# Bounding a MoE-style layer's weights with products of TensorE, and giving their halves three free places

## The chip, the core and the metric

The kernel runs on one core of a Trainium2 chip. TensorE (PE) multiplies, VectorE (DVE) and ScalarE (ACT) do elementwise work and reductions, GpSimd (POOL) does elementwise work too, SyncE (SP) issues the DMAs. The metric is the time of one execution in microseconds (us).

## What is computed

```python
q_n, k_n, c_n = q, k, centroids divided by (their norms + 1e-6)
q_assign = argmax(q_n . c_n);  k_assign = argmax(k_n . c_n)      # 16 clusters per head
scores = where(q_assign == k_assign, (q @ k.T) / sqrt(D), -1e9)
attn   = softmax(scores)
x      = (attn @ v) laid out as (B*S, H*D) = (3072, 512)
r      = maximum(x @ moe_w_in, 0)                                # moe_w_in (512, 2048), float64
out    = (s * r * r + b) @ moe_w_out                             # moe_w_out (2048, 512), float64
```

B = 4, H = 8, S = 768, D = 64. Attention within clusters, then a two-layer MLP with a squared Relu. The weights and `s`, `b` lie in memory as 64-bit floats, so each weight is two 32-bit words.

## The kernel before

The work is a list of 192 attention **units** (one batch, one chunk of 256 queries, one pair of heads, one of two query tiles, one head) and 192 **MLP steps** (batch, chunk, one of 16 slices `ft` of the hidden layer). Unit `i` makes scores on TensorE (`scores`, L454), their maximum on VectorE (`maxima`, L463, tile `ssm`), the exponentials on ScalarE (`exps`, L473, tile `p`), the 16-bit high and low parts `ph` (L119 or L121, and L496 on GpSimd), a transpose by DMA (`PT`), and for each pair of units the product with the values (`values`, L515 to L517, tile `px`), then normalised into `xs` (L527). The first 8 units have no low part and are turned by TensorE (`turned`, L493). MLP step `m` runs 21 units behind (`LAG`): `mlp_in` (L573, tile `h`), `mlp_relu` (L580 to L583, tiles `r`, `g`), `mlp_gl` (L588), `mlp_out` (L600, tile `acc`). `mlp_start` computes per chunk a scale `cf` (L562) from the largest `xs`; each Relu needs it.

The products run in 16 bit with every operand split in a high and a low part, and for the weights that needs a bound first. The weights come in 32 **halves** of 128 x 512 numbers (`wi0`, `wo0`, `wi1`, `wo1`, ... `wo15`; even ones from `moe_w_in`, odd ones from `moe_w_out`). The generator `weights` moves each half through these steps, two per unit:

- `fetch`: DMA of 512 KB into a staging tile `wst`, one of three; the next load into the same tile waits until the half in it is joined.
- `rebase` (ScalarE, L203): makes a 32-bit float out of the high words, short of three bits.
- `narrow` (VectorE): shifts these words left by three (L207) and joins the top three bits of the low words (L208).
- `bound`: ScalarE writes the absolute values in 16 bit (`wab`, L215 or L217). For odd halves it also sums them by row (`l1`). For even halves TensorE multiplies them by ones (`pw`, L220), which sums the columns, and VectorE takes the largest (`w1`, L221).

`finish_w_in` and `finish_w_out` make scales in `glob` out of the bounds. Then `wsplit(ft)` splits each half into a 16-bit high part on ScalarE (L265, tiles `wis`, `wos`) and a low part on VectorE (L267). The split goes into a new place of the ring of `weight_tile`, and the place of the unsplit half is free only once its low part is made. The ring has 33 places for 32 halves.

Within each engine instructions run in the order of a list that a scheduler writes when the program is built, on its own estimates of durations; the first 20 units have a raised priority. So a change of one operation can move others in these lists.

Of the kernel before, what the change touches and what calls it, by code (L numbers as in the profile page):

```python
# [9 lines left out]
BF16 = mybir.dt.bfloat16  # L10
F32 = mybir.dt.float32
I32 = mybir.dt.int32
U32 = mybir.dt.uint32
AF = mybir.ActivationFunctionType
ALU = mybir.AluOpType
AX = mybir.AxisListType
# [10 lines left out]
def tile_cluster_attention_mlp(ctx, tc, q, k, v, cent, w_in, w_out, s_in, b_in, out):  # L27
# [28 lines left out]
    def const(shape, dt, name):  # L56
        return cp.tile(shape, dt, tag=name, name=name)

    def floor2(eng, dst, src):
        eng.tensor_scalar(dst, src, 2.0 ** -60, 2.0 ** 60, op0=ALU.max, op1=ALU.min)  # L60
        eng.tensor_scalar(dst.bitcast(I32), dst.bitcast(I32), EXPMASK, None, op0=ALU.bitwise_and)

    def inverse2(eng, dst, src, e):
        eng.tensor_scalar(dst.bitcast(I32), src.bitcast(I32), -1, (254 + e) << 23, op0=ALU.mult, op1=ALU.add)
# [25 lines left out]
    def columns(n, name):  # L90
        return sb.tile([P, n], BF16, tag=f"amb{n}", name=f"amb_{name}", bufs=3)
# [12 lines left out]
    rev = const([P, C], F32, "rev")  # L104
    for c in range(C):
        G.memset(rev[:, c : c + 1], float(C - c))
    ones = const([P, P], BF16, "ones")
    G.memset(ones, 1.0)
    ident = const([P, P], F32, "ident")
    G.memset(ident, 1.0)  # L110
    G.affine_select(ident, ident, pattern=[[1, P]], base=0, channel_multiplier=-1, compare_op=ALU.is_equal, fill=0.0)
    identb = const([P, P], BF16, "identb")
# [53 lines left out]
    WSP = {}  # L166

    def weight_tile(name):
        return cp.tile([P, KT, P], F32, tag="w", name=name, bufs=2 * NF + 1)
    w1 = const([P, NF], F32, "w1")  # L170
    l1 = const([P, NF], F32, "l1")
    glob = const([P, 12], F32, "glob")
    bias = []

# [26 lines left out]
    def rebase(d):  # L201
        hw = d["st"][:, :, :, 1].bitcast(F32)
        A.activation(d["w"], hw, AF.Prelu, scale=2.0 ** -112, alpha=-(2.0 ** 32))  # L203

    def narrow(d):
        c = d["w"].bitcast(I32)
        V.tensor_scalar(c, c, 3, None, op0=ALU.logical_shift_left)  # L207
        V.scalar_tensor_tensor(c.bitcast(U32), d["st"][:, :, :, 0].bitcast(U32), 29, c.bitcast(U32),  # L208
                               op0=ALU.logical_shift_right, op1=ALU.bitwise_or)

    def bound(d):
        w, p, ft = d["w"], d["p"], d["ft"]
        wa = sb.tile([P, KT, P], BF16, tag="wab", name=f"wab_{p}", bufs=2)
        if p % 2:
            A.activation(wa, w, AF.Abs, accum_out=l1[:, ft : ft + 1])  # L215
        else:
            A.activation(wa, w, AF.Abs)  # L217
            pw = ps_h.tile([P, 512], F32, tag="h", name=f"pw_{ft}")
            for t in range(KT):
                nc.tensor.matmul(pw[:, :P], ones, wa[:, t, :], start=(t == 0), stop=(t == KT - 1))  # L220
            V.tensor_reduce(w1[:, ft : ft + 1], pw[:, :P], axis=AX.X, op=ALU.max)  # L221
        if ft == NF - 1:
            (finish_w_out if p % 2 else finish_w_in)()

    narrowed = [0]

    def weights():
        live = {}
        for i in range(2 * NF + 3):
            if 0 <= i - 3:  # L230
                bound(live[i - 3])
                narrowed[0] += 1
            if 0 <= i - 2 < 2 * NF:
                rebase(live[i - 2])
                narrow(live[i - 2])
            if i < 2 * NF:
                live[i] = fetch(i)
            if i < 2 * NF + 2:
                yield

    def finish_w_in():
        V.tensor_reduce(glob[:, 0:1], w1, axis=AX.X, op=ALU.max)
        V.tensor_scalar(glob[:, 0:1], glob[:, 0:1], 1.02, None, op0=ALU.mult)
        floor2(V, glob[:, 1:2], glob[:, 0:1])
        inverse2(V, glob[:, 2:3], glob[:, 1:2], 0)
        V.tensor_scalar(glob[:, 2:3], glob[:, 2:3], 2.0 ** 13, None, op0=ALU.mult)
        V.tensor_scalar(glob[:, 1:2], glob[:, 1:2], 2.0 ** -7, None, op0=ALU.mult)

    def finish_w_out():
        lc = columns(1, "w")  # L250
        V.tensor_reduce(lc, l1, axis=AX.X, op=ALU.max)
        allmax(glob[:, 4:5], lc, "w")
        floor2(V, glob[:, 4:5], glob[:, 4:5])
        inverse2(V, glob[:, 5:6], glob[:, 4:5], 0)
        V.tensor_scalar(glob[:, 5:6], glob[:, 5:6], 2.0 ** 13, None, op0=ALU.mult)
        V.tensor_scalar(glob[:, 4:5], glob[:, 4:5], 2.0 ** -13, None, op0=ALU.mult)
        V.tensor_tensor(glob[:, 6:7], sv, glob[:, 4:5], op=ALU.mult)

    def wsplit(ft):
        while narrowed[0] < 2 * NF:  # L260
            next(wgen)
        made = []
        for w, f in ((wi[ft], glob[:, 2:3]), (wo[ft], glob[:, 5:6])):
            e = parts(weight_tile(f"w{'io'[len(made)]}s{ft}"))
            A.activation(e[:, 0], w, AF.Copy, scale=f)  # L265
            yield
            V.scalar_tensor_tensor(e[:, 1], w, f, e[:, 0], op0=ALU.mult, op1=ALU.subtract)  # L267
            made.append(e)
        WSP[ft] = (made[0], made[1].rearrange("p e a f -> p e (a f)"))
# [489 lines left out]
```

## Time and profile before

| | |
|---|---|
| three runs | 954.69 us median (954.56 to 957.88) |
| profiled execution | 959.63 us, its span 957.6 us |
| busy TensorE / VectorE / ScalarE / GpSimd | 831.2 / 614.9 / 709.9 / 568.9 us |
| first half rebased, last half joined | 22.9 us, 132.2 us |
| first Relu of the MLP | 160.8 us |
| last split's start on VectorE | 226.0 us |
| MLP alone on TensorE, at the end | from about 890 us |

Times count from the start of the span. The start of the kernel (to 132 us) fills the weights' places and runs the first 17 units beside it; the rest alternates units and MLP steps on TensorE.

### The profile page before, as it was taken

Reading aid. Unit: us, or ns where it says so; the run is one execution under the profiler, and the core shown is the slowest. Engines: PE = TensorE matmul, PEld = TensorE weight load, DVE = VectorE, ACT = ScalarE, POOL = GpSimd, SP = SyncE. Lnnn points to the kernel's source line nnn. Section 1 sums busy time; section 2 is a strip of 40 time slices with the busy share of each in tenths; the row PEclk is TensorE's granted clock in tenths of the full one; section 3 lists DMA queues with packets and bytes.
Section 4 is the critical chain, followed back from the end, with each engine's and each line's share of the span. In section 5 each row is a group of like instructions: output and inputs, shape, how many; then the busy total and the mean of one; then the engine's idle time right before and its main releaser. Section 6 shows DMA issues by size and latency. Waiting matters only on the chain. (4 is left out here: it accounts for less than half of the span.)

```text
span 957.6 us, 22486 instructions
## 1 busy us (share of the span) xinstructions
PE 831.2 (87%) x8625; PEld 580.0 (61%) x8625; DVE 614.9 (64%) x1400; ACT 709.9 (74%) x1390; POOL 568.9 (59%) x596
## 2 busy tenths in 40 slices
PE   1668446988899999987999999998899999999997
PEld 0456323655567776655676676665666766767664
DVE  8797978888767746566856555487775466463100
ACT  4477656978579888866887988786888888889443
POOL 4012545868468667656676756666776765676321
PEclk9966657999999999999999999999999999999999
DMA  7887974688677777799887757889787866676200
GB/s 187 218 217 217 256 170 94 156 180 152 142 157 165 167 139 163 131 182 197 163 157 152 160 129 162 160 184 207 142 172 154 149 112 150 138 158 138 33 24 22
DMA packets 450299, 147.36 MB, mean 154 GB/s; under 512 B 417936, under 2 KB 446608, under 8 KB 450192
## 3 DMA queue, kind: packets, MB, share of 16 engines
q1 hardware_dynamic: 450192, 145.93, 72.0%
q8 instruction: 67, 1.10, 0.5%
q14 instruction: 40, 0.33, 0.1%
HBM read 35.69 MB, written 6.29 MB: 44 GB/s over the span
## 5 line engine op out<-in xcount | busy, mean ns | idle before, releaser
L496 POOL TENSOR_TENSOR ph<-p,ph 128x768 f16<-128x768 f32 x184 | 314.2, 1707 | 123.7 <-ACT ph L119 82.7
L600 PE MATMUL acc<-wos,g 128*128 128x512 f16 x1152 | 298.5, 381 | 5.0 <-POOL g L588 4.6
L573 PE MATMUL h<-x,wis 128*128 128x256 f16 x2304 | 290.2, 275 | 8.4 <-ACT r L580 4.1
L573 PEld LDWEIGHTS <-wis 128*128 128x128 f16 x2304 | 223.3, 98 | 62.7 <-issue 10.3
L463 DVE TENSOR_REDUCE ssm<-sc 128x1 f32<-128x768 f32 x192 | 181.2, 951 | 30.1 <-PE sc L454 29.5
L588 POOL TENSOR_TENSOR g<-r,g 128x256 f16<-128x256 f32 x192 | 131.9, 688 | 110.0 <-ACT r L583 106.3
L473 ACT ACTIVATE p<-sc,ssm,qsm 128x768 f32<-128x768 f32 x192 | 188.0, 979 | 2.6 <-POOL g L588 0.4
L600 PEld LDWEIGHTS <-g 128*128 128x128 f16 x1152 | 103.8, 98 | 87.9 <-POOL g L588 10.3
L580 ACT ACTIVATE r<-h,cf 128x256 f32<-128x256 f32 x192 | 89.4, 466 | 77.0 <-PE h L573 62.1
L119 ACT ACTIVATE ph<-p 128x768 f16<-128x768 f32 x164 | 136.3, 831 | 9.1 <-DMA PT<-ph 8.7
L515 PE MATMUL px<-vh,PT 128*128 128x65 f16 x1104 | 119.6, 196 | 10.8 <-DVE xs L527 4.6
L470 ACT ACTIVATE ssm<-ssm,lift,qsm 128x1 f32<-128x1 f32 x192 | 73.2, 381 | 74.5 <-DVE ssm L463 73.4
L516 PE MATMUL px<-vl,PT 128*128 128x64 f16 x1104 | 119.6, 193 | 0.0
L517 PE MATMUL px<-vh,PT 128*128 128x65 f16 x1104 | 119.6, 194 | 0.0
L454 PE MATMUL sc<-KA,QA 128*128 128x384 f16 x384 | 99.8, 342 | 20.4 <-ACT p L473 17.4
L515 PEld LDWEIGHTS <-PT 128*128 128x128 f16 x1104 | 103.6, 98 | 18.5 <-issue 8.9
L516 PEld LDWEIGHTS <-PT 128*128 128x128 f16 x1104 | 103.2, 100 | 13.7 <-issue 5.3
L454 PE MATMUL sc<-KB,QB 128*128 128x384 f16 x384 | 100.4, 344 | 8.7 <-DMA QB<-qb 8.7
L517 PEld LDWEIGHTS <-PT 128*128 128x128 f16 x1104 | 103.5, 98 | 3.4
L582 ACT ACTIVATE g<-r 128x256 f16<-128x256 f32 x192 | 79.3, 413 | 3.6
L583 ACT ACTIVATE r<-r 128x256 f32<-128x256 f32 x192 | 78.8, 410 | 3.1
L523 DVE TENSOR_SCALAR ssm<-px 128x2 f32<-128x2 f32 x92 | 14.3, 155 | 79.9 <-PE px L517 79.8
(156 smaller groups left out, 1039.9 us busy)
## 6 DMA issues: line engine op xcount, KB each, us to landing
wst<-in_moe_w_in_dram SPq DMA_DIRECT2D x16, 512.0 KB, 4.9
wst<-in_moe_w_out_dram SPq DMA_DIRECT2D x16, 512.0 KB, 4.6
kn<-in_k_dram SPq DMA_DIRECT2D x16, 384.0 KB, 3.9
qn<-in_q_dram SPq DMA_DIRECT2D x24, 256.0 KB, 3.6
vn<-in_v_dram SPq DMA_DIRECT2D x16, 384.0 KB, 5.0
out_dram<-o SPq DMA_DIRECT2D x12, 512.0 KB, 3.7
PT<-ph SPq DMA_TRANSPOSE x184, 3.4
x<-xn SPq DMA_TRANSPOSE x48, 2.5
```

The source lines that it names most:

```text
L119: A.activation(dst, src, AF.Copy)
L454: last_score[0] = nc.tensor.matmul(sc[:, e, :HALF], X[:, col, :], y[:, h * S + e * HALF : h * S + (e + 1) * HALF], start=st, stop=not st)
L463: last_max[0] = V.tensor_reduce(SM[i // 4][:, 0, j : j + 1], U[i]["sc"], axis=AX.XY, op=ALU.max, negate=True)
L473: last_exp[0] = A.activation(p.rearrange("p (a b) -> p a b", a=2), u["sc"], AF.Exp, bias=bi, scale=u["scale"], **total)
L496: G.tensor_tensor(u["ph"][:, 1, :], u["p"], u["ph"][:, 0, :], op=ALU.subtract)
L515: nc.tensor.matmul(o1, PT[:, kt, :], vh[:, h, kt, : D + 1], start=(kt == 0), stop=False)
L516: nc.tensor.matmul(o, PT[:, kt, :], vl[:, h, kt, :], start=False, stop=False)
L517: nc.tensor.matmul(o1, PT[:, T + kt, :], vh[:, h, kt, : D + 1], start=False, stop=(kt == T - 1))
L573: nc.tensor.matmul(ph[:, :CW], WSP[ft][0][:, wl, kt, :], XS[(b, c, kt)][:, :, xl, :], start=(i == 0), stop=(i == len(terms) - 1))
L580: A.activation(r, ph[:, :CW], AF.Relu, scale=MS[(b, c)][0])
L588: G.tensor_tensor(g[:, 1, :], r, g[:, 0, :], op=ALU.subtract)
L600: nc.tensor.matmul(acc[:, t, :], g[:, gl, rows], WSP[ft][1][:, wl, :], start=(ft == 0 and gl + wl == 0), stop=(ft == NF - 1 and gl == 1))
```

## The change

The low words' three bits are now made by ScalarE, in place in the staging tile: it reads the word as an unsigned number, scales it by 0.9375 * 2^-29, subtracts 1/32 and writes an integer. VectorE then needs one instruction for shift and join. The bound comes no longer from absolute values: TensorE multiplies each 128 x 128 block of a half with itself, reading the upper 16 bits of each 32-bit weight as a bfloat16 number, summed over the half's four blocks. The largest entry of such a product is the largest sum of squares of a column. This is done for four halves at a time, in one PSUM tile, and VectorE takes four maxima (`wsq`) in one instruction. `wab`, `ones`, `w1` and `l1` are gone, `ident` lives in the ring of `g`, and the weights' ring has 35 places. `finish_weights` takes the roots of both bounds at the end.

```diff
-    ones = const([P, P], BF16, "ones")
-    G.memset(ones, 1.0)
-    ident = const([P, P], F32, "ident")
+    ident = sb.tile([P, P], F32, tag="g", name="ident", bufs=4)
...
-        return cp.tile([P, KT, P], F32, tag="w", name=name, bufs=2 * NF + 1)
-    w1 = const([P, NF], F32, "w1")
-    l1 = const([P, NF], F32, "l1")
+        return cp.tile([P, KT, P], F32, tag="w", name=name, bufs=2 * NF + 3)
+    wsq = const([P, NF, 2], F32, "wsq")
...
     def rebase(d):
         hw = d["st"][:, :, :, 1].bitcast(F32)
         A.activation(d["w"], hw, AF.Prelu, scale=2.0 ** -112, alpha=-(2.0 ** 32))
+        lw = d["st"][:, :, :, 0]
+        A.activation(lw, lw.bitcast(U32), AF.Copy, scale=0.9375 * 2.0 ** -29, bias=-0.03125)

     def narrow(d):
         c = d["w"].bitcast(I32)
-        V.tensor_scalar(c, c, 3, None, op0=ALU.logical_shift_left)
-        V.scalar_tensor_tensor(c.bitcast(U32), d["st"][:, :, :, 0].bitcast(U32), 29, c.bitcast(U32),
-                               op0=ALU.logical_shift_right, op1=ALU.bitwise_or)
-
-    def bound(d):
-        w, p, ft = d["w"], d["p"], d["ft"]
-        wa = sb.tile([P, KT, P], BF16, tag="wab", name=f"wab_{p}", bufs=2)
-        if p % 2:
-            A.activation(wa, w, AF.Abs, accum_out=l1[:, ft : ft + 1])
-        else:
-            A.activation(wa, w, AF.Abs)
-            pw = ps_h.tile([P, 512], F32, tag="h", name=f"pw_{ft}")
+        V.scalar_tensor_tensor(c.bitcast(U32), c.bitcast(U32), 3, d["st"][:, :, :, 0].bitcast(U32),
+                               op0=ALU.logical_shift_left, op1=ALU.bitwise_or)
+
+    def bound(four):
+        pw = ps_h.tile([P, 512], F32, tag="h", name=f"pw_{four[0]['ft']}")
+        for j, d in enumerate(four):
+            wa = d["w"].bitcast(BF16).rearrange("p a (f z) -> p a f z", z=2)[:, :, :, 1]
             for t in range(KT):
-                nc.tensor.matmul(pw[:, :P], ones, wa[:, t, :], start=(t == 0), stop=(t == KT - 1))
-            V.tensor_reduce(w1[:, ft : ft + 1], pw[:, :P], axis=AX.X, op=ALU.max)
-        if ft == NF - 1:
-            (finish_w_out if p % 2 else finish_w_in)()
+                nc.tensor.matmul(pw[:, j * P : (j + 1) * P], wa[:, t, :], wa[:, t, :], start=(t == 0), stop=(t == KT - 1))
+        ft = four[0]["ft"]
+        V.tensor_reduce(wsq[:, ft : ft + 2, :], pw.rearrange("p (f e q) -> p f e q", e=2, q=P), axis=AX.X, op=ALU.max)
+        if ft + 2 == NF:
+            finish_weights()
...
         for i in range(2 * NF + 3):
-            if 0 <= i - 3:
-                bound(live[i - 3])
+            p = i - 3
+            if p >= 0 and p % 4 == 3:
+                bound([live[p - 3 + j] for j in range(4)])
+            if p >= 0:
                 narrowed[0] += 1
...
+    def finish_weights():
+        lc = columns(2, "w")
+        V.tensor_reduce(lc, wsq.rearrange("p f e -> p e f"), axis=AX.X, op=ALU.max)
+        allmax(glob[:, 8:10], lc, "w")
+        root = glob[:, 8:10].bitcast(I32)
+        V.tensor_scalar(glob[:, 8:9], glob[:, 8:9], float(DM), None, op0=ALU.mult)
+        V.tensor_scalar(glob[:, 8:10], glob[:, 8:10], 1.04, None, op0=ALU.mult)
+        V.tensor_scalar(root, root, 1, None, op0=ALU.logical_shift_right)
+        V.tensor_scalar(root, root, 127 << 22, None, op0=ALU.add)
...
```

The scheduler's lists move too. First VectorE in the weights' stage, around halves 8 to 10, before (the number behind a name tells the half, unit or staging load; the last number is only the buffer's):

```order
L207 TENSOR_SCALAR wo8_848<-wo8_848 128x512
L221 TENSOR_REDUCE w1_128<-pw_7_839 128x1
L208 SCALAR_TENSOR_TENSOR wo8_848<-wst_17_849,wo8_848 128x512
L207 TENSOR_SCALAR wi9_856<-wi9_856 128x512
L208 SCALAR_TENSOR_TENSOR wi9_856<-wst_18_857,wi9_856 128x512
L207 TENSOR_SCALAR wo9_900<-wo9_900 128x512
L208 SCALAR_TENSOR_TENSOR wo9_900<-wst_19_901,wo9_900 128x512
L207 TENSOR_SCALAR wi10_908<-wi10_908 128x512
L463 TENSOR_REDUCE ssm_8_864<-sc_11_1021 128x1
L208 SCALAR_TENSOR_TENSOR wi10_908<-wst_20_909,wi10_908 128x512
```

and the same place in the new list:

```order
L206 SCALAR_TENSOR_TENSOR wo8_821<-wo8_821,wst_17_822 128x512
L458 TENSOR_REDUCE ssm_8_853<-sc_11_998 128x1
L206 SCALAR_TENSOR_TENSOR wi9_845<-wi9_845,wst_18_846 128x512
L522 TENSOR_TENSOR xs_1_919<-px_6_1012,ssm_4_636 128x128
L206 SCALAR_TENSOR_TENSOR wo9_881<-wo9_881,wst_19_882 128x512
L216 TENSOR_REDUCE wsq_126<-pw_8_938 128x4
L101 TENSOR_REDUCE xm_0_814<-xs_1_919 128x1
L458 TENSOR_REDUCE ssm_12_1070<-sc_12_1063 128x1
L206 SCALAR_TENSOR_TENSOR wi10_887<-wi10_887,wst_20_888 128x512
```

One instruction per half stands where two stood, and unit work has moved into the gaps.

Second, ScalarE behind the last half, where the splits begin, before:

```order
L265 ACTIVATE wis0_1440<-wi0_256,glob_130 128x512
L470 ACTIVATE ssm_16_1360<-ssm_16_1360,lift_132,qsm_0_1_0_829 128x1
L473 ACTIVATE p_17_1384<-sc_17_1375,ssm_16_1360,qsm_0_1_0_829 128x768
L265 ACTIVATE wos0_1463<-wo0_259,glob_130 128x512
L265 ACTIVATE wis1_1465<-wi1_265,glob_130 128x512
```

and now:

```order
L260 ACTIVATE wis0_1420<-wi0_253,glob_127 128x512
L260 ACTIVATE wos0_1443<-wo0_256,glob_127 128x512
L260 ACTIVATE wis1_1445<-wi1_262,glob_127 128x512
L260 ACTIVATE wos1_1503<-wo1_391,glob_127 128x512
L260 ACTIVATE wis2_1505<-wi2_397,glob_127 128x512
```

The high parts stand in a row. Third, VectorE where the first chunk's `cf` is made out of `xm_0`, before:

```order
L98 TENSOR_REDUCE xm_0_833<-am_x3_1576 128x1
L121 CAST ph_19_1535<-p_19_1476 128x768
L290 TENSOR_REDUCE om_q0_1_1_1562<-oe_q0_1_1_1563 128x8
L558 TENSOR_SCALAR xm_0_833<-xm_0_833,glob_130 128x1
L291 TENSOR_TENSOR oo_q0_1_1_1564<-oe_q0_1_1_1563,om_q0_1_1_1562 128x128
L60 TENSOR_SCALAR xm_0_833<-xm_0_833 128x1
L267 SCALAR_TENSOR_TENSOR wos4_1708<-wo4_626,glob_130,wos4_1708 128x512
L61 TENSOR_SCALAR xm_0_833<-xm_0_833 128x1
L64 TENSOR_SCALAR xm_0_833<-xm_0_833 128x1
L562 TENSOR_SCALAR cf_0_0_1596<-xm_0_833,glob_130 128x1
```

and now:

```order
L61 TENSOR_SCALAR xm_0_814<-xm_0_814 128x1
L519 RECIPROCAL ssm_16_1340<-ssm_16_1340 128x2
L458 TENSOR_REDUCE ssm_20_1517<-sc_23_1694 128x1
L262 SCALAR_TENSOR_TENSOR wis11_2149<-wi11_959,glob_127,wis11_2149 128x512
L64 TENSOR_SCALAR xm_0_814<-xm_0_814 128x1
L522 TENSOR_TENSOR xs_4_1640<-px_16_1601,ssm_16_1340 128x128
L262 SCALAR_TENSOR_TENSOR wos11_2243<-wo11_989,glob_127,wos11_2243 128x512
L262 SCALAR_TENSOR_TENSOR wis12_2245<-wi12_995,glob_127,wis12_2245 128x512
L458 TENSOR_REDUCE ssm_24_1800<-sc_24_1787 128x1
L557 TENSOR_SCALAR cf_0_0_1576<-xm_0_814,glob_127 128x1
```

Ahead of `cf` stand the low parts up to `wis12` where they stood up to `wos4`, and the maxima up to unit 24 where they stood up to unit 21.

More of the change, by code (lines that the diff above doesn't have):

```diff
@@ L239, in weights @@
                 yield
[L241 to L256, printed above, removed]
+    def finish_weights():
[7 more added lines that the diff above has]
+        V.tensor_scalar(root, root, 127 << 22, None, op0=ALU.add)
+        V.tensor_copy(glob[:, 0:1], glob[:, 8:9])
+        floor2(V, glob[:, 8:10], glob[:, 8:10])
+        inverse2(V, glob[:, 10:12], glob[:, 8:10], 13)
+        V.tensor_scalar(glob[:, 1:2], glob[:, 8:9], 2.0 ** -7, None, op0=ALU.mult)
+        V.tensor_scalar(glob[:, 4:5], glob[:, 9:10], 2.0 ** -13, None, op0=ALU.mult)
         V.tensor_tensor(glob[:, 6:7], sv, glob[:, 4:5], op=ALU.mult)
@@ L262, in wsplit @@
         made = []
-        for w, f in ((wi[ft], glob[:, 2:3]), (wo[ft], glob[:, 5:6])):
+        for w, f in ((wi[ft], glob[:, 10:11]), (wo[ft], glob[:, 11:12])):
             e = parts(weight_tile(f"w{'io'[len(made)]}s{ft}"))
```

## The prediction

> **What bounds the kernel now.** I read the page first: the engines' busy time, then the slices over the span.
>
> ```profile
> span 957.6 us, 22486 instructions
> PE 831.2 (87%) x8625; PEld 580.0 (61%) x8625; DVE 614.9 (64%) x1400; ACT 709.9 (74%) x1390; POOL 568.9 (59%) x596
> PE   1668446988899999987999999998899999999997
> DVE  8797978888767746566856555487775466463100
> PEclk9966657999999999999999999999999999999999
> ```
>
> TensorE is full from about slice 8; ahead of it VectorE is the busy one, and TensorE's granted clock is near half. All that the change touches lies there. So I cut the start into stages by busy time (columns: length, then PE, PEld, DVE, ACT, POOL with counts, granted clock, DMA share, GB/s).
>
> ```profile
> 24.00:44.00 20.00, 11.60 (x109) 8.02 (x107) 14.19 (x34) 7.88 (x16) 0.04 (x1) 1.00 0.84 185
> 44.00:132.00 88.00, 53.13 (x372) 40.73 (x371) 75.89 (x154) 61.40 (x123) 30.79 (x28) 0.63 0.90 238
> 132.00:160.00 28.00, 15.53 (x160) 9.79 (x159) 23.79 (x63) 15.72 (x27) 12.27 (x11) 0.64 0.37 83
> 160.00:228.00 68.00, 60.82 (x633) 41.33 (x634) 60.45 (x118) 57.52 (x117) 49.88 (x41) 1.00 0.77 163
> 228.00:912.00 684.00, 647.70 (x7061) 452.69 (x7060) 419.35 (x968) 537.65 (x1049) 455.86 (x460) 0.99 0.76 152
> ```
>
> 44 to 132 is the weights' stage: VectorE 86% busy, DMA share 0.90, TensorE idle 35 us of 88. 132 to 160 waits for the first MLP step, VectorE 85% busy. From 160 TensorE is the bound. What happens in the first two stages moves the end one for one, as TensorE's remaining work (about 748 us of 831) starts later or sooner.
>
> Inside the weights' stage I follow one of the 32 halves round its loop: load, ScalarE's rebase (L203), VectorE's shift (L207) and join (L208), and then the load three halves on, which takes the same staging buffer.
>
> ```profile
> DMA to landing us min/median/max: 3.3/4.7/7.2
> 44.17 0.68 ACT L203 ACTIVATE wo<-wst 128x512 f32<-128x512 f32 x1 [1.99 <-DMA wst<-in_moe_w_out_dram]
> 130.38 0.66 ACT L203 ACTIVATE wo<-wst 128x512 f32<-128x512 f32 x1 [1.39 <-DMA wst<-in_moe_w_out_dram]
> L207 DVE TENSOR_SCALAR wi<-wi 128x512 int32<-128x512 int32 x16 | 8.9, 557 | 4.4 <-ACT wi L203 4.4
> L207 DVE TENSOR_SCALAR wo<-wo 128x512 int32<-128x512 int32 x16 | 7.2, 450 | 3.7 <-ACT wo L203 3.7
> L208 DVE SCALAR_TENSOR_TENSOR wi<-wst,wi 128x512 uint32<-128x512 uint32 x16 | 16.9, 1053 | 0.1
> L208 DVE SCALAR_TENSOR_TENSOR wo<-wst,wo 128x512 uint32<-128x512 uint32 x16 | 13.5, 841 | 0.1
> SPq L85 <- DVE wo L208: 19.9, 9, 3.8
> SPq L85 <- DVE wi L208: 11.5, 6, 2.3
> ```
>
> From the rebase of half 3 (44.17) to that of half 31 (130.38) are 28 halves in 86.2 us, 3.08 us each; with three buffers one turn of the loop takes 9.24 us. The groups' means give 4.7 (landing) + 0.67 + 0.50 (shift) + 0.95 (join) = 6.8, so 2.4 us a turn is standing in queues. SP's queue stood 31.4 us waiting for a join, in 15 waits: the load is mostly held by VectorE, which has to be reached twice in a turn.
>
> **The change, part by part.** Prices of what goes and of the nearest rows for what comes:
>
> ```profile
> L215 ACT ACTIVATE wab<-wo 128x512 bf16<-128x512 f32 x16 | 10.0, 624 | 2.8 <-DVE wo L208 2.7
> L217 ACT ACTIVATE wab<-wi 128x512 bf16<-128x512 f32 x16 | 10.0, 624 | 6.2 <-DVE wi L208 4.8 <-DVE ssm L523 1.1
> L220 PE MATMUL pw<-wab,ones 128*128 128x128 bf16 x64 | 9.5, 295 | 11.8 <-ACT wab L217 7.5 <-DVE w L221 2.5 <-DVE oe_k L287 1.9
> 44.00:132.00 88.00, 14.86 (x29) 0.63 0.90 238
> 44.00:132.00 88.00, 4.22 (x15) 0.63 0.90 238
> L101 DVE TENSOR_REDUCE amb_q<-qn 128x2 bf16<-128x512 f32 x24 | 16.4, 684 | 35.1 <-DMA qn<-in_q_dram 34.9
> ```
>
> The fourth and fifth rows are VectorE's busy time in the weights' stage for L207 and for L221.
>
> VectorE there: minus 14.86 (shifts), minus 4.22 (one-column maxima), plus seven maxima over 128x512 at 0.68 (row L101, of that size): 14.3 us less. ScalarE: minus 32 Abs at 0.62, plus 32 low-word copies that no row shows; between 0.62 (Abs) and 0.72 (the split's copy), I take 0.67, the rebase reading the same strided words. Sum 21.4 against 20: nothing, and ScalarE is idle 27 of 88 us. But the copy joins the chain and the Abs leaves ScalarE's queue, where it waited for the joins (2.7 and 4.8 us) with the next rebase behind it.
>
> TensorE: 64 products of 128 columns more, 9.5 us if a strided read costs as a dense one (row L220; from 0 to twice that); TensorE's 35 idle us hide them unless they stand ahead of something urgent, the second rival. SP's queue keeps its order but for swaps of neighbours; no load passes a transpose, no DMA is added. POOL loses one memset. `ident` in the ring of `g` is free before step 3 needs the place: nothing.
>
> *Stage 24 to 44:* three shifts and one maximum less on VectorE (1.5 us) among the one-hot steps that the first transposes wait for; minus 1 (0 to minus 1.5).
>
> *Weights' stage.* New turn: 4.7 + 0.67 + 0.67 + 0.95 = 7.0, plus queues. One pass through VectorE's queue in place of two, in a queue less full (86% to about 70%): 1.4 us in place of 2.4. Turn 8.4, 2.80 us a half, 28 halves: **minus 8**. Ends: nothing gained (queues 2.25), and minus 14.3 (VectorE's whole saving). I stay in the middle because the loop also holds the landing, SP's transposes and a DMA share of 0.90, which at minus 8 reaches 0.99.
>
> *From the last join to the first Relu.* Here the extra places act.
>
> ```profile
> 131.54 0.69 DVE L208 SCALAR_TENSOR_TENSOR wo<-wst,wo 128x512 uint32<-128x512 uint32 x1
> 158.78 0.21 DVE L562 TENSOR_SCALAR cf<-xm,glob 128x1 f32<-128x1 f32 x1
> 160.77 0.46 ACT L580 ACTIVATE r<-h,cf 128x256 f32<-128x256 f32 x1
> 132.00:160.00 28.00, 8.96 (x11) 0.64 0.37 83
> 160.00:228.00 68.00, 18.15 (x22) 1.00 0.77 163
> 132.00:160.00 28.00, 3.81 (x4) 0.64 0.37 83
> ACT wis L265 <- DVE wos L267: 9.1, 5, 2.6
> ACT wos L265 <- DVE wis L267: 6.3, 7, 2.6
> ```
>
> (The two rows with x11 and x22 are VectorE's lower halves of the weights, L267; the one with x4 its score maxima, L463.) With one free place ScalarE and VectorE took turns, ScalarE waiting 15.4 us; three places end that wait. But VectorE is the busy engine, and in the new order 25 of the 32 lower halves stand ahead of `cf`, without which no Relu starts, where 10 stood; with them seven score maxima in place of four. Before, join to `cf` was 27.3 us, holding 8.96 of lower halves, 3.81 of maxima, 11.0 of others and 4.2 idle. After: 25 x 0.815 = 20.4, 7 x 0.95 = 6.7, others 14 (a pair of px more, a cast, the last wide maximum, both finishes behind the last join), 3 idle: 44 us. **Plus 16.7** (38 to 48, with lower halves at 0.73 without neighbours or the old idle: plus 10.7 to 20.7).
>
> *What is given back.*
>
> ```profile
> L454 PE MATMUL sc<-KB,QB 128*128 128x384 f16 x384 | 100.4, 344 | 8.7 <-DMA QB<-qb 8.7
> L515 PE MATMUL px<-vh,PT 128*128 128x65 f16 x1104 | 119.6, 196 | 10.8 <-DVE xs L527 4.6 <-DVE xm L98 1.8 <-DVE qsm L98 1.5
> 161.00:281.00 120.00, 107.81 (x1085) 71.58 (x1082) 96.40 (x199) 91.06 (x179) 80.51 (x75) 0.97 0.75 154
> 260.00:270.00 10.00, 6.40 (x51) 3.82 (x52) 7.41 (x16) 4.63 (x9) 6.03 (x7) 0.83 0.57 123
> 300.00:400.00 100.00, 97.97 (x1069) 68.86 (x1068) 61.21 (x139) 83.87 (x167) 69.76 (x69) 1.00 0.73 148
> ```
>
> At the second MLP step TensorE then has two units' scores (four matmuls of 0.26) and half a pair's values (18 of 0.108) behind it that came later before: **minus 4**. And from the first Relu VectorE is rid of nearly all lower halves (18.15 of its 60.45 us): of TensorE's 12.2 idle us in 161 to 281 there stay the 2% of a calm stretch (2.4, last row) and the dip at 260 for the next chunk (3.6); of the other 6.2 I take **minus 5.5** (minus 2 to minus 9.8, the dip gone too). After about step 8 both orders run side by side, so the rest keeps its time.
>
> **Sum:** -1 - 8 + 16.7 - 4 - 5.5 = -1.8, say minus 2. The profiled execution took 959.63 us (span 957.6 and 2.03 around it), 4.9 above the median of 954.69; applied to the median: **952.7**.
>
> **A rule and the trace.** The granted clock was 0.63 in the weights' stage with TensorE 60% busy, and 1.00 from 160 on with it 89% busy. The Trainium skill, "TensorE: Matmul & The Clock Gate", Part 1, says that activity releases the throttle, after a window of some 3.4 us of sustained work; the trace agrees as far as it goes. By that rule bursts of 16 products could bring the full clock into the weights' stage, which makes the third rival.
>
> **The rivals.**
>
> *VectorE alone paces the loop* (faster). For it: 86% busy, and 14 us of its work goes. Against: DMA share 0.90. Then -14.3 stands for -8: sum -8.1, **946.6**. It becomes faster than 0.5% once the stage yields 11.
>
> *The bursts hold the units* (slower). One group of 16 products now waits in TensorE's queue for the join of its fourth half, 2.4 us long in place of 0.6 (0.148 each).
>
> ```profile
> PE pw L220 <- ACT wab L217: 7.5, 3, 4.5
> ```
>
> Small groups already cost waits up to 4.5 us. Behind the first burst stand the second turn of unit 1's probabilities, and then scores, maxima, exps, the probability transposes in SP's queue, and behind those the next load. Seven bursts at 1.2 us more each would eat the 8: sum +6.2, **960.9**. It decides when the stage yields under 1.4. Against: TensorE idles 35 us there.
>
> *The clock comes up early* (faster). Half of those 7.5 us at most, 3.7: **949.0**. Against: 9.5 us on 53 leave it at about 70% busy, in bursts shorter than the gaps.
>
> *The places do nothing.* If ScalarE's wait just turns into a wait for VectorE's queue, the order still holds, and the 16.7 with it; this is inside the forecast.
>
> **How the numbers follow.** 0.5% (4.8 us) is about what a measurement tells from no change. My forecast, within that, 0.40; VectorE paces 0.31 and the clock 0.05, together faster 0.36; the bursts 0.24. The bounds added up reach from -19 to +15; eight in ten lie about halfway out from the sum: 944.5 to 961. The likeliest case's own range is 950 to 959.4.
>
> **What would show it.** The rebases of halves 3 to 31 spaced 2.8 us; SP's waits for joins well under 31 us; the last join near 123; `cf` some 44 us behind it, near 166; the last lower half near 177 in place of 226; TensorE idle under 7 us in the 120 us after the first Relu. Wrong it is if the loop yields far from 8, or if `cf` comes less than 38 us after the last join, since the sum is a small difference of large terms.

## The result, and the profile after

| | before | after |
|---|---|---|
| median of the compared runs | 955.46 us (953.87 to 957.88, 6 runs) | 964.98 us (959.42 to 967.30, 6 runs) |
| ratio | | 1.0065, interval 1.0041 to 1.0088 |
| profiled execution, its span | 959.63, 957.6 us | 965.81, 964.1 us |

The change makes the kernel slower, clear of the noise. How much is less sure: the ratio on record is worth 6.2 us and its interval ends at 8.4, while the two medians of the table differ by 9.5 us. The spans of the two profiled executions differ by 6.5 us, and what follows explains these 6.5. First the page of the kernel after: span, busy time, and the slices over the span.

```profile
span 964.1 us, 22519 instructions
PE 835.6 (87%) x8690; PEld 583.7 (61%) x8690; DVE 600.6 (62%) x1358; ACT 710.2 (74%) x1374; POOL 567.6 (59%) x595
PE   0577554899799999999899999998899999999997
DVE  7677669858487646557867656576767566463100
```

VectorE lost 14.3 us of work, as the change meant. But in the seventh slice (145 to 169 us) TensorE, which stood at 6 before, stands at 4, and VectorE, which stood at 8, at 9: where TensorE's work should begin, VectorE is fuller than before. The stages by busy time (columns as before):

```profile
24.00:44.00 20.00, 11.04 (x123) 7.62 (x121) 13.43 (x31) 7.76 (x17) 0.30 (x2) 1.00 0.83 190
44.00:132.00 88.00, 55.10 (x442) 41.75 (x441) 60.07 (x116) 60.78 (x110) 31.60 (x29) 0.70 0.93 243
132.00:160.00 28.00, 14.44 (x146) 9.25 (x145) 26.77 (x59) 20.86 (x34) 13.38 (x10) 0.56 0.32 71
160.00:228.00 68.00, 56.57 (x553) 38.31 (x551) 52.37 (x105) 46.69 (x93) 37.49 (x34) 0.89 0.62 142
```

In the weights' stage VectorE is 60.07 us busy instead of 75.89; from 132 to 160 it is nearly full, 26.77 of 28, and from 160 to 228 TensorE does 56.57 us of work where it did 60.82.

The loop: rebase of half 3, of half 31, the last join, what SyncE's queue waited for, and the two new kinds of instruction (least, median and largest ns).

```profile
43.85 0.68 ACT L200 ACTIVATE wo<-wst 128x512 f32<-128x512 f32 x1 [1.23 <-DMA wst<-in_moe_w_out_dram]
128.72 0.66 ACT L200 ACTIVATE wo<-wst 128x512 f32<-128x512 f32 x1 [3.11 <-DMA wst<-in_moe_w_out_dram]
129.96 0.69 DVE L206 SCALAR_TENSOR_TENSOR wo<-wo,wst 128x512 uint32<-128x512 uint32 x1 [1.08 <-ACT wst L202]
SPq L85 <- DVE wo L206: 12.3, 8, 3.0
SPq L85 <- DVE wi L206: 7.6, 3, 3.5
L202 ACT ACTIVATE wst<-wst x32: 634/652/682, 23.9 to 129.3; 128x512 int32<-128x512 uint32 x32
L214 PE MATMUL pw<-wi x64: 218/292/315, 44.4 to 125.8; 128*128 128x128 bf16 x64
```

From half 3 to half 31 are 28 halves in 84.9 us, 3.03 us each, against 3.08 before. The last join ends at 130.65 instead of 132.23: the stage yields 1.6 us. Yet SyncE's queue stood only 19.9 us for joins, not 31.4. The copy costs 0.652 us, the strided product 0.292, both as estimated.

Then `cf`, the first and the last Relu of the MLP; VectorE's lower halves (L262) and score maxima (L458) from 132 to 170; and TensorE (first number after the length) in the window that the prediction quoted:

```profile
169.99 0.20 DVE L557 TENSOR_SCALAR cf<-xm,glob 128x1 f32<-128x1 f32 x1
171.39 0.46 ACT L575 ACTIVATE r<-h,cf 128x256 f32<-128x256 f32 x1
955.86 0.47 ACT L575 ACTIVATE r<-h,cf 128x256 f32<-128x256 f32 x1 [1.24 <-PE h L568]
...
132.00:170.00 38.00, 24.59 (x25) 0.59 0.41 88
132.00:170.00 38.00, 6.56 (x7) 0.59 0.41 88
...
161.00:281.00 120.00, 101.69 (x998) 67.10 (x997) 86.89 (x188) 78.42 (x151) 67.19 (x65) 0.93 0.63 140
```

`cf` comes 40.0 us after the start of the last join, where it came 27.2 us after it. The first Relu is 10.6 us later than before (160.77), the last 6.5 us later (949.38 before). So the 6.5 us are -1.6 (last join), +12.2 (from the join's start to the first Relu: 41.4 us instead of 29.2) and -4.1 (from the first Relu to the last: 784.5 us instead of 788.6).

### The profile page after: what moved, and what is told of

Read it like the earlier page. It is cut to its first block, busy times and chain, and to the rows that moved or that the text cites. A ratio compares the mean times of both kernels' runs of the same rounds, so it can differ in the third digit from the quotient of the medians.

```text
span 964.1 us, 22519 instructions
## 1 busy us (share of the span) xinstructions
PE 835.6 (87%) x8690; PEld 583.7 (61%) x8690; DVE 600.6 (62%) x1358; ACT 710.2 (74%) x1374; POOL 567.6 (59%) x595
## 5 line engine op out<-in xcount | busy, mean ns | idle before, releaser
L458 DVE TENSOR_REDUCE ssm<-sc 128x1 f32<-128x768 f32 x192 | 181.3, 952 | 33.5 <-PE sc L449 33.0
L510 PE MATMUL px<-vh,PT 128*128 128x65 f16 x1104 | 122.0, 198 | 10.0 <-DVE qsm L98 3.7
L511 PE MATMUL px<-vl,PT 128*128 128x64 f16 x1104 | 122.0, 195 | 0.0
L512 PE MATMUL px<-vh,PT 128*128 128x65 f16 x1104 | 121.7, 196 | 0.0
L449 PE MATMUL sc<-KA,QA 128*128 128x384 f16 x384 | 101.3, 347 | 17.0 <-ACT p L468 14.1
L511 PEld LDWEIGHTS <-PT 128*128 128x128 f16 x1104 | 104.7, 101 | 16.2 <-issue 8.7
L510 PEld LDWEIGHTS <-PT 128*128 128x128 f16 x1104 | 105.0, 99 | 13.3 <-issue 3.6
L512 PEld LDWEIGHTS <-PT 128*128 128x128 f16 x1104 | 105.0, 99 | 3.2 <-issue 0.2
L518 DVE TENSOR_SCALAR ssm<-px 128x2 f32<-128x2 f32 x92 | 14.3, 155 | 80.9 <-PE px L512 80.7
```

Of the source, the lines that this page charges most:

```text
L449: last_score[0] = nc.tensor.matmul(sc[:, e, :HALF], X[:, col, :], y[:, h * S + e * HALF : h * S + (e + 1) * HALF], start=st, stop=not st)
L458: last_max[0] = V.tensor_reduce(SM[i // 4][:, 0, j : j + 1], U[i]["sc"], axis=AX.XY, op=ALU.max, negate=True)
L510: nc.tensor.matmul(o1, PT[:, kt, :], vh[:, h, kt, : D + 1], start=(kt == 0), stop=False)
L511: nc.tensor.matmul(o, PT[:, kt, :], vl[:, h, kt, :], start=False, stop=False)
L512: nc.tensor.matmul(o1, PT[:, T + kt, :], vh[:, h, kt, : D + 1], start=False, stop=(kt == T - 1))
```

## Experiments on the free places

Each ratio below is to the kernel before, run beside it on the same chip, with its interval. The times of single events are from the one profiled execution of each kernel.

**One free place, all else as changed.**

```diff
-        return cp.tile([P, KT, P], F32, tag="w", name=name, bufs=2 * NF + 3)
+        return cp.tile([P, KT, P], F32, tag="w", name=name, bufs=2 * NF + 1)
```

> The changed kernel with one free place for the weights' halves in place of three; low words, join and products stay. Theory A (the places: with three, 25 low halves stand ahead of cf in VectorE's list and the first MLP step comes 11 us late; here 8 stand ahead of it): last join near 130.5 us as with three, cf within 26 to 30 us behind it, first Relu near 159, time 951 to 955 us, so 8 to 12 under the changed kernel. Theory B (the groups of 16 products hold up the units and cost the time): no more than 3 us under the changed kernel, 959 or more.

Measured 958.34 us (955.57 to 959.93), ratio 0.9999 (0.9978 to 1.0019). `cf` and the first Relu in its timeline:

```profile
156.01 0.21 DVE L557 TENSOR_SCALAR cf<-xm,glob 128x1 f32<-128x1 f32 x1
157.74 0.46 ACT L575 ACTIVATE r<-h,cf 128x256 f32<-128x256 f32 x1
```

Without the two further places the loss is gone: the first Relu is 13.7 us earlier than with them, 3.0 earlier than before. And the rest of the change, 14 us less work on VectorE, is worth nothing at the end: by MLP step 16 the Relu is 5.1 us later than before (240.2 against 235.1), and the last Relus fall together (949.2 and 949.4).

**The kernel before with three places.** `wab`, `ones` and `ident` move into rings that are not in use yet, which makes the room.

```diff
-        return cp.tile([P, KT, P], F32, tag="w", name=name, bufs=2 * NF + 1)
+        return cp.tile([P, KT, P], F32, tag="w", name=name, bufs=2 * NF + 3)
...
-        wa = sb.tile([P, KT, P], BF16, tag="wab", name=f"wab_{p}", bufs=2)
+        wa = sb.tile([P, KT, P], BF16, tag="r", name=f"wab_{p}", bufs=2)
... (ones and ident go into the ring of g)
```

> The kernel before with three free places for the weights' halves; nothing else of the change, but wab lies in the ring of r, ones and ident in the ring of g, to make room. 29 low halves stand ahead of the first cf in VectorE's list. Theory A (the places let VectorE's list fill with low halves before they are needed): last join near 132 us, first Relu 8 to 14 us later than 160.8, time 959 to 967 us, 4 to 9 over the kernel before. Rival (the places harm only together with the products or the low words): within 2 us of the kernel before.

Measured 962.61 us (961.65 to 967.94), ratio 1.0066 (1.0040 to 1.0092). The last join and the first Relu:

```profile
131.12 0.69 DVE L208 SCALAR_TENSOR_TENSOR wo<-wst,wo 128x512 uint32<-128x512 uint32 x1
172.13 0.46 ACT L580 ACTIVATE r<-h,cf 128x256 f32<-128x256 f32 x1
```

The places alone, with the old bound and the old shift and join, cost what the whole change costs, and make the first Relu as late. With the run before, this shows that the slowdown belongs to the places: taken out of the changed kernel they take it away, and put into the kernel before they bring it. How it gets from the first Relu to the end is less clear, as the next two runs show.

**Two free places.**

```diff
-        return cp.tile([P, KT, P], F32, tag="w", name=name, bufs=2 * NF + 3)
+        return cp.tile([P, KT, P], F32, tag="w", name=name, bufs=2 * NF + 2)
```

> The changed kernel with one more free place than before instead of two more (bufs=2*NF+2), all else as after. Theory A (each free place beyond the first lets a split's high half be made earlier and so puts its low half, 0.74 us and more on VectorE, ahead of the scores' maxima and of the products with the values between 135 and 190 us; the loss is a dose): first Relu between 157.7 (one place) and 171.4 us (three places), near 164, last Relu near 952.5, time 960 to 963, ratio 1.002 to 1.006. Rival (it is a threshold: the lists change only where three splits run ahead, or the loss is an accident of one list): two places stand with one, first Relu within 2 us of 157.7 and ratio within 0.002 of 1, or already all of it (1.0065).

Measured 955.34 us (952.69 to 959.94), ratio 0.9991 (0.9975 to 1.0006): no change, where a part of the loss was expected.

```profile
161.69 0.46 ACT L575 ACTIVATE r<-h,cf 128x256 f32<-128x256 f32 x1
```

Lower halves that stand ahead of `cf` in VectorE's list, against the first Relu and the ratio:

| kernel | lower halves ahead of `cf` | first Relu | ratio |
|---|---|---|---|
| changed, one place | 8 | 157.7 us | 0.9999 |
| before | 10 | 160.8 us | 1 |
| changed, two places | 16 | 161.7 us | 0.9991 |
| changed, three places | 25 | 171.4 us | 1.0065 |
| before, three places | 29 | 172.1 us | 1.0066 |

In these five the first Relu follows the lower halves. The end does not follow it step by step: the second place costs 4 us at the first Relu and nothing at the end. Some of that came back far behind the change (from MLP step 96 to step 112 took 67.9 us, with one place 71.3), and why is open. Nor is an early first Relu enough: two kernels further down, the products alone and the smaller bursts, have 8 lower halves ahead of `cf` and a first Relu at 158.7 and 156.6 us, and their ratios are 1.0062 and 1.0037.

**Three places, lower halves behind `cf`.** The lower halves of slice 4 and up are put behind the first `cf` in VectorE's list; the upper halves still run ahead.

```diff
...
-            V.scalar_tensor_tensor(e[:, 1], w, f, e[:, 0], op0=ALU.mult, op1=ALU.subtract)
+            with behind(first_cf[0] if ft >= 4 else None):
+                V.scalar_tensor_tensor(e[:, 1], w, f, e[:, 0], op0=ALU.mult, op1=ALU.subtract)
... (first_cf is set where the first cf is made)
```

> The changed kernel with its three places, but the low halves from slice 4 on are queued on VectorE behind the first cf. Theory A (it is the order, not the places themselves): first Relu between 156 and 160 us, time 950 to 955 us, as with one place or a little less, since ScalarE may run three high halves ahead. Theory B (products): 959 or more, first Relu early all the same.

Measured 962.66 us (958.81 to 967.95), ratio 1.0055 (1.0031 to 1.0078). Its first Relu and that of MLP step 8, and the windows behind the first Relu, this kernel first, then before, then after:

```profile
156.73 0.46 ACT L579 ACTIVATE r<-h,cf 128x256 f32<-128x256 f32 x1
199.52 0.47 ACT L579 ACTIVATE r<-h,cf 128x256 f32<-128x256 f32 x1
...
160.00:170.00 10.00, 7.22 (x76) 4.65 (x74) 9.90 (x17) 8.99 (x18) 5.61 (x5) 1.00 0.44 105
170.00:180.00 10.00, 6.80 (x92) 4.55 (x93) 9.93 (x20) 7.76 (x16) 3.87 (x4) 1.00 0.42 93
180.00:190.00 10.00, 6.90 (x59) 4.25 (x55) 9.93 (x16) 8.96 (x19) 6.62 (x6) 1.00 0.45 103
```

```profile
160.00:170.00 10.00, 9.23 (x91) 6.40 (x92) 7.71 (x14) 9.65 (x21) 7.01 (x5) 1.00 0.68 140
170.00:180.00 10.00, 8.63 (x90) 6.02 (x88) 9.82 (x20) 8.52 (x18) 7.95 (x6) 1.00 0.59 131
180.00:190.00 10.00, 9.91 (x107) 6.61 (x106) 8.99 (x15) 9.76 (x21) 8.41 (x8) 1.00 0.84 162
```

```profile
160.00:170.00 10.00, 5.19 (x62) 3.50 (x60) 10.00 (x21) 7.21 (x12) 4.42 (x4) 0.67 0.66 133
170.00:180.00 10.00, 7.24 (x45) 4.11 (x43) 10.00 (x18) 9.55 (x20) 5.85 (x5) 0.92 0.35 79
```

This was the instructive failure. The first Relu is 4 us earlier than before, so `cf` is cured, and the loss stays. VectorE is full from 160 to 190 us (9.9 of each 10): 17 lower halves start there, where 9 did before. TensorE, which needs score maxima and scaled values from VectorE, does 20.9 us of work where it did 27.8; step 8's Relu is 7.5 us later than before (192.0). So it is not `cf` alone that the crowd delays. With one place the ring spaces the lower halves: each needs its upper half, and that needs the place which the lower half before it gives back (9 from 160 to 190 us with one place too, in the changed kernel). With three nothing in the ring does. Two points stay open. With two places 15 lower halves start in that window and VectorE is nearly as full (9.6, 9.8 and 9.9 of 10), but TensorE does 25.7 us there and the end is not later. And that spacing them with three places in hand would bring the time back was not tried.

## Experiments on the weights' stage

**The two parts of the lighter loop, one at a time.** First (in the cut) the kernel before with ScalarE's low words and the single join, old bound; then the changed kernel with one place, the products, and the old shift and join.

```diff
 def rebase(d):
+        lw = d["st"][:, :, :, 0]
+        A.activation(lw, lw.bitcast(U32), AF.Copy, scale=0.9375 * 2.0 ** -29, bias=-0.03125)
... (narrow as in the change)
```

> The kernel before with the low words' bits made by ScalarE and one join on VectorE; bound by Abs and ones, one free place. Theory A (the weights' stage is held by SP's queue and the DMAs, not by VectorE): the last join comes 0 to 3 us sooner than 132.2 us, time 952 to 956 us. Theory B (VectorE paces the loop, and in the changed kernel the products' bursts ate the gain): last join near 124 to 126, time 947 to 950 us.

> The changed kernel's bound by products, with the shift and join of before on VectorE, and one free place. Theory A: the last join within 2 us of 132.2, time 953 to 957 us. Theory B (bursts hold the units): last join near 138, time 959 to 963 us.

Low words alone: 961.79 us (957.25 to 965.32), ratio 1.0046 (1.0026 to 1.0066); last join 135.5 us, later than before, with ScalarE 72.96 us busy of 88 (61.40 before). Products alone: 962.29 us (960.47 to 966.12), ratio 1.0062 (1.0036 to 1.0087); last join 132.2 us, as before. Neither makes the loop shorter. The low words' loss begins in this stage: their first Relu comes at 165.8 us, 5.1 later than before. That of the products does not show in the start of the trace (first Relu 158.7), and its profiled execution was the fastest of its nine. That each alone costs half a per cent, and both together nothing, stays open; it also means that a loss of this size is no mark of the places.

**Smaller bursts.** One place, and the products of each half issued by themselves, four in a row instead of sixteen.

```diff
-            if p >= 0 and p % 4 == 3:
-                bound([live[p - 3 + j] for j in range(4)])
             if p >= 0:
+                bound(live[p])
... (bound fills a quarter of a PSUM tile, with the maxima behind the fourth)
```

> The changed kernel with one free place, and the products of each half made as soon as it is joined, four at a time, in place of sixteen at a time behind the fourth half. Theory S (SP's queue and the DMAs hold the weights' stage): last join within 2 us of the 131.2 with sixteen, time within 2 us of that kernel. Theory B (the bursts hold the units, and through them the transposes ahead of the loads): last join 4 us or more sooner, time 3 to 6 us less. A difference in the list of the order may blur 2 us.

Measured 960.10 us (955.16 to 969.34), ratio 1.0037 (1.0010 to 1.0064); last join 130.1 us. TensorE's waits for joins in the stage fell from 21.1 us with one place to 14.1, and the last join came 1.1 us sooner: the bursts are not what held the stage. The time was to be that of one place (0.9999) and is longer; why is open.

**The loads on another queue.** One place; the weights' loads are issued by GpSimd, and in a second kernel by ScalarE, so that they no longer stand among the attention's transposes on SyncE's queue.

```diff
-        load(st.rearrange("p a f w -> p a (f w)"), src)
+        nc.gpsimd.dma_start(st.rearrange("p a f w -> p a (f w)"), src)    # or nc.scalar
```

> The changed kernel with one free place, and the weights' loads issued from GpSimd's queue, so that they stand behind no transpose in SP's queue. Theory S (SP's queue order is what holds the loop now): the last join comes 6 to 12 us sooner than 131.2, near 120 to 125; the time falls by about half of it, since the list then also puts the joins ahead of two units. Theory D (the DMA engines are full, share 0.93): the last join comes within 3 us of 131, and a load takes longer to land than 4.7 us.

> As the kernel with loads from GpSimd's queue, but from ScalarE's queue, where a load's wait for a join also stops ScalarE. Theory S: last join sooner than 131.2 by 4 to 12 us, with ScalarE's waits for joins up; time lower only if these waits stay under the gain. Theory D: last join within 3 us of 131.

GpSimd: 964.52 us (958.68 to 971.11), ratio 1.0073 (1.0047 to 1.0099), last join 127.5 us, 3.7 sooner than with SyncE's queue, where 6 to 12 or under 3 were expected. ScalarE: 968.88 us (966.31 to 975.66), ratio 1.0132 (1.0095 to 1.0169). ScalarE's version, half 3's join, the last one, and the exponentials of unit 16:

```profile
34.03 0.69 DVE L206 SCALAR_TENSOR_TENSOR wo<-wo,wst 128x512 uint32<-128x512 uint32 x1 [2.82 <-ACT wst L202]
116.97 1.88 DVE L206 SCALAR_TENSOR_TENSOR wo<-wo,wst 128x512 uint32<-128x512 uint32 x1 [0.17 <-ACT wst L202]
139.31 0.97 ACT L468 ACTIVATE p<-sc,ssm,qsm 128x768 f32<-128x768 f32 x1
```

On ScalarE's queue the last join comes 12 us earlier than with one place and SyncE's, and the units pay for it: unit 16 is at 139.3 instead of 130.7 us, the first Relu at 168.2 instead of 157.7. The pace is still 3.0 us a half (84.1 us for 28); only the start is earlier.

**The same in the kernel before.** Here, too, ScalarE issues the loads; nothing else differs from the kernel before.

> The kernel before with one line changed: the weights' loads are issued from ScalarE's queue and not from SyncE's. With the same line in the changed kernel with one place the last join came at 119 us instead of 131. Theory S (SyncE's queue, where the loads stand behind the attention's own transposes, sets the turn of the loop; VectorE's two instructions do not): here too the last join comes near 120 us, within 2 us of the other, and the shift and the bound's maximum that the change saves are worth nothing there either. Rival V (VectorE is next in line behind the queue): the last join stays above 125 us, and the difference to 119 is what the change's lighter VectorE would be worth once the queue is out of the way. Either way the first units come later (first p near 48 us instead of 36), the first Relu is near 168 us, and the time is 1.005 to 1.015 of before.

Measured 976.11 us (970.76 to 979.15), ratio 1.0202 (1.0177 to 1.0227). The joins of half 3 and the last:

```profile
37.31 0.69 DVE L208 SCALAR_TENSOR_TENSOR wo<-wst,wo 128x512 uint32<-128x512 uint32 x1
121.64 0.68 DVE L208 SCALAR_TENSOR_TENSOR wo<-wst,wo 128x512 uint32<-128x512 uint32 x1
```

The last ends at 122.3 us, 3.5 us behind the changed kernel under the same condition, which lies between the two expectations, nearer to that of the queue. But 3.3 of these 3.5 us are there at half 3 already (34.03 against 37.31). From there to the last join the two kernels run at the same pace, 84.1 and 84.3 us: VectorE's 14 us are worth next to nothing to the loop here either, and as the pace stays at 3.0 us a half without SyncE's queue, that queue alone does not set it. The first Relu comes at 182.1 us, where 168 was expected, with 18 lower halves ahead of `cf` (11 in the changed kernel); the time misses its range of 1.005 to 1.015 with it.

**Half the bytes.** From half 3 on only 256 KB of each half are loaded, in the changed kernel with one place and in the kernel before; the other 256 KB of the staging tile keep what stood there. To that end the three staging tiles leave their ring and stand fixed, and the output tile `o` shares them.

```diff
-        st = sb.tile([P, KT, P, 2], I32, tag="stage", name=f"wst_{p}", bufs=3)
-        load(st.rearrange("p a f w -> p a (f w)"), src)
+        st = staged[p % 3]
+        if p < 3:
+            load(st.rearrange("p a f w -> p a (f w)"), src)
+        else:
+            load(st[:, : KT // 2].rearrange("p a f w -> p a (f w)"), src[:, : KT // 2])
...
```

> The changed kernel with one place, but from half 3 on only the first 256 KB of each half's 512 KB are loaded (the rest of the staging tile keeps old numbers, so half of the weights are wrong; all instructions on the engines stay). In seven kernels so far the loop ran at 2.9 to 3.2 us per half, whoever issued the loads and whatever VectorE carried, with a DMA share of 0.86 to 0.94. Theory D (the transfers set the pace): from half 3 to half 31 the joins are spaced under 2.6 us, the last join is before 120 us in place of 131, the DMA share in 44 to 132 falls under 0.8. Theory Q (the engines' lists set it: the halves' rebase, copy and join stand in line with the units' work, two halves per unit, and SyncE's loads behind the units' transposes): spacing 2.8 to 3.05 us, last join 126 to 132 us, and only the DMA share falls. First Relu moves with the last join at most.

> The same edit in the kernel before (256 KB of each half loaded from half 3 on, the rest of the staging tile old numbers). Theory D: as in the changed kernel the spacing falls under 2.6 us; what is then left of a difference between the two kernels is what the lighter VectorE is worth once the transfers are out of the way, at most the 14 us of its saved work, by my forecast about 8. Theory Q: 2.9 to 3.1 us as before, last join near 131, no difference to the other beyond 2 us.

953.54 us (949.45 to 956.16), ratio 0.9980 (0.9955 to 1.0004), and 956.95 us (948.60 to 962.54, 9 runs), ratio 1.0011 (0.9978 to 1.0044). The changed kernel with half loads: the weights' stage, and the joins of halves 3, 20, 21 and 31; then halves 3, 20 and 31 of the one with one place and full loads:

```profile
44.00:132.00 88.00, 55.29 (x458) 41.34 (x457) 69.30 (x127) 61.28 (x112) 32.85 (x30) 0.69 0.61 159
45.06 0.69 DVE L211 SCALAR_TENSOR_TENSOR wo<-wo,wst 128x512 uint32<-128x512 uint32 x1 [0.79 <-ACT wst L207]
84.18 1.38 DVE L211 SCALAR_TENSOR_TENSOR wi<-wi,wst 128x512 uint32<-128x512 uint32 x1
97.58 1.31 DVE L211 SCALAR_TENSOR_TENSOR wo<-wo,wst 128x512 uint32<-128x512 uint32 x1
126.72 0.68 DVE L211 SCALAR_TENSOR_TENSOR wo<-wo,wst 128x512 uint32<-128x512 uint32 x1
```

```profile
44.94 0.69 DVE L206 SCALAR_TENSOR_TENSOR wo<-wo,wst 128x512 uint32<-128x512 uint32 x1 [0.93 <-ACT wst L202]
95.79 0.68 DVE L206 SCALAR_TENSOR_TENSOR wi<-wi,wst 128x512 uint32<-128x512 uint32 x1
130.54 0.69 DVE L206 SCALAR_TENSOR_TENSOR wo<-wo,wst 128x512 uint32<-128x512 uint32 x1 [1.05 <-ACT wst L202]
```

The DMA share falls from 0.90 to 0.61, and up to half 20 the pace is 2.34 us a half instead of 2.99 (in the kernel before 2.49 instead of 2.98). Up to there the bytes are part of what sets the turn, and with half of them VectorE's relief shows: half 20 is joined at 85.6 us, in the kernel before at 87.8.

Then comes one gap: half 21 is joined 13.4 us behind half 20, in the kernel before 16.6. In the changed kernel its load (86.55 us) stood in SyncE's queue behind the transpose of a unit, which waited 7.6 us for GpSimd, and its rebase (95.93) in ScalarE's list behind work of the units that waited for TensorE and VectorE. From half 21 to half 31 the pace is 2.91 us, with full loads 3.26. Of the 10.9 us gained by half 20 only 3.8 are left at the last join. So over all 28 halves, 2.92 us each, the rival expectation of the lists came out, and up to half 20 that of the transfers. At full loads, too, the queue delays the last load. SyncE's own queue, before and then after, the last rows up to the load of half 31:

```profile
121.19 3.55 SPq L498 DMA_TRANSPOSE PT<-ph  x1
124.79 0.57 SPq L85 DMA_DIRECT2D qn<-in_q_dram  x1
125.47 0.44 SPq L85 DMA_DIRECT2D wst<-in_moe_w_out_dram  x1
```

```profile
120.25 3.13 SPq L493 DMA_TRANSPOSE PT<-ph  x1
123.43 0.57 SPq L85 DMA_DIRECT2D qn<-in_q_dram  x1
124.10 0.45 SPq L85 DMA_DIRECT2D wst<-in_moe_w_out_dram  x1
```

The load of half 31 stands behind the transpose of a unit's probabilities, and comes when that unit is ready: its staging tile was free at 124.0 and 120.8 us, the load came at 125.5 and 124.1. Where the loads stay in this queue the last join ends beside the exponentials of unit 16: joins at 132.2, 130.7, 127.4 and 134.6 us (before, after, and the two with half loads), unit 16 at 131.3, 130.1, 127.1 and 134.6. What paces the units there was not isolated.

## Why the prediction was wrong

Forecast no change (952.7 us), range to 961.0; measured 964.98. By the steps of its sum:

- **Weights' stage, -8; measured -1.6.** This step failed. Its parts were right: copy 0.652 us against 0.67, VectorE's relief in the stage 15.8 us against 14.3. What was wrong was to call SyncE's 31.4 us of waits for joins proof that VectorE holds the load. The waits shrank by 11.5 us, and the last load came 1.4 us sooner. By the timelines, averaged over halves 4 to 31, the way from a rebase to the end of its join fell by 0.59 us a turn (3.52 to 2.94), but the way from a load's issue to its rebase grew by 0.27 (5.05 to 5.32) and that from a join to the next load into its tile by 0.13 (1.55 to 1.68). So 0.19 us a turn was left, 1.7 us for 28 halves with three tiles. Part of what took it back is the queue: the last five loads came on average 2.5 us behind the join that freed their tile, before 1.2. Part is the transfers: with half the bytes the pace fell, and VectorE's relief was worth 2.3 us at half 20. Neither alone sets the pace; what paces the units is open. The lower bound, nothing gained, stood in the range of the term, for queues that fill up again; the measurement lies near it.
- **Last join to first Relu, +16.7; measured +12.8 to `cf`, +12.2 to the Relu.** The mechanism held, shown by taking the places away and by adding them alone. 25 lower halves stood ahead of `cf`, at 0.98 us each, not 0.815; the maxima cost 6.56 us (6.7 said); what was too large is the other work and the idle, 8.9 us together where 17 were put down. `cf` came 40.0 us behind the join, inside 38 to 48. (The 27.3 us before were filled with rows of the 28 us from 132 to 160, which hold an eleventh lower half, behind `cf`; that slip is under 1 us.)
- **Given back, -4 and -5.5; measured -4.1 together, and not by that mechanism.** This failed too. The argument was that VectorE, rid of the lower halves, would feed TensorE better from the first Relu on. But the crowd lasts beyond it: VectorE is full to 180 us and the Relu of step 8 is 14.4 us late (206.4 against 192.0), later than the first. In the 120 us behind its own first Relu TensorE idles 13.5 us, where under 7 were said and 12.2 stood before (18.3 in the fixed window 161 to 281). At step 128 the kernel is still 10.0 us late, and the 4 us come back between there and step 160 (6.3 us late), far behind the change; why is open. That this size is near the first of the two terms is luck. The run with `cf` ahead of the crowd shows the same crowd without the late `cf`.
- **One for one.** The sum also took what happens ahead of the first Relu as moving the end one for one. It does not: against the kernel before, the first Relu and the last moved by -3.0 and -0.1 us with one place, by +0.9 and -3.9 with two, by -4.0 and +3.1 with `cf` first, by +10.6 and +6.5 in the changed kernel. What levels them out is open.
- **The sum.** -1.6 + 12.2 - 4.1 = +6.5, against -1.8. The stage 24 to 44 is inside the first term: half 3 was rebased 0.3 us earlier, where 1 was put down.
- **The rivals.** The slower one gave about the right time, +6.2, by luck: it had the bursts hold the units, and smaller bursts brought nothing. Its condition, a stage that yields under 1.4, was nearly met. That of the clock came about in part by its column, 0.70 in place of 0.63 in the stage (how far that column can be trusted stands in the last section), and can have brought no more than part of the 1.6 us.

## What to carry to other kernels

Ask what spaces a row of work that nobody needs yet: a scarce buffer may be the only thing that does, and with more buffers a scheduler may put that work ahead of what the critical engine waits for, as it did here. Take a queue's waits for an engine as what ended last, not as time that a faster engine gives back: look at what stands next in the same queue and at the share of the transfers, and count the gain only if both leave room. A forecast that is the difference of a gain in one stage and a loss in the next should be checked stage by stage for its weakest term; here both gains were the weak ones. And a stage that ends earlier is not yet a kernel that ends earlier: follow a late event to the end before it is counted in full.

## What the hardware showed that was not expected

The granted clock in the records is not always the speed of the products. In the kernel before with loads on ScalarE's queue it reads 1.00 from 54 to 104 us, in the kernel before 0.50 to 0.67; the 32-bit products of the values take the same time in both. Rows: a window, and the group of those products from 54 to 104 us (busy, mean ns), first with ScalarE's loads, with the 16-bit scores of the same stretch, then before.

```profile
84.00:94.00 10.00, 3.94 (x32) 2.70 (x31) 8.56 (x18) 7.86 (x14) 1.37 (x2) 1.00 0.79 210
L510 PE MATMUL px<-vn,PT 128*128 128x64 f32 x69 | 15.5, 414 | 0.1
L454 PE MATMUL sc<-KA,QA 128*128 128x384 f16 x16 | 6.7, 512 | 3.8 <-ACT p L473 3.8
```

```profile
84.00:94.00 10.00, 9.63 (x49) 8.86 (x49) 6.82 (x12) 7.14 (x14) 2.69 (x2) 0.50 0.88 223
L510 PE MATMUL px<-vn,PT 128*128 128x64 f32 x72 | 16.2, 415 | 0.0
```

Busy time for one is the same too, 0.225 us. The scores say more: at 1.00 they take 512 ns and 0.42 us of busy time each, while from 300 to 400 us, at 1.00 as well, the same products take 326 ns and 0.25 us in both kernels. So the products from 54 to 104 us run slower than the column says.

The Trainium skill, "TensorE: Matmul & The Clock Gate", Part 1, warns that on trn2 the trace events of the clock gate have been seen to be unreliable; 414 ns at 1.00 and 415 ns at 0.50 to 0.67 agree with that warning. So in the start of this kernel the clock's column carries no argument by itself.

Besides, VectorE's join is 0.69 us at its median, but up to 2.15 us in the kernel before, 1.79 us after and 2.16 us with half loads; nothing in these runs separates what lengthens it.
